# Query tiles 4 to 6 turned by DMA, and the last output tile stored in three pieces

## The chip, the cores and the metric

The program runs on one core of one Trainium2 chip. A core has a tensor engine (PE, with its weight loads shown apart as PEld), a vector engine (DVE), a scalar engine (ACT), a pool engine (POOL) and a sync engine (SP), which in this kernel only issues DMAs. Each engine works through its own list of instructions in order and waits on semaphores where it needs another engine's result. The metric is the device time of one execution in microseconds; lower is better.

## The reference

One transformer layer on 2048 tokens of width 576, in bfloat16. Cut to what matters:

```
x  = A_x                                   # 1 x 2048 x 576
q, k, v = layernorm(x) @ wq, wk, wv        # 32 heads of width 18
for s in range(4):                         # four segments of 512 tokens
    p     = softmax(q_s k_s^T / sqrt(18) + causal mask)
    a_dot = p v_s
    a_mem = phi(q_s) M / (phi(q_s) z + 1e-6)     # phi(t) = t + 1 if t > 0 else exp(t)
    o_s   = g a_mem + (1 - g) a_dot              # g = sigmoid(beta), one gate per head
    M, z += phi(k_s)^T v_s, sum(phi(k_s))
h   = x + o @ wo
out = h + gelu(layernorm(h) @ w1 + b1) @ w2 + b2  # 576 -> 4608 -> 576
```

## The kernel before

Tokens are cut into 16 tiles of 128 rows, and two tiles make a chunk (8 chunks of 256). Tile t of chunk c is t = 2c + tl. For each tile the kernel loads x, normalises it (statistics and scaling on DVE, the power of -1/2 on POOL), turns it so that the width lies on partitions, projects it to q, k and v (L984), copies the results out of PSUM with padding to 32 columns per head (L988 to L1008), and turns q and k again (the tiles QT and KT). Attention goes in "visits": scores for four units into one PSUM tile (L1109, 32-row tiling of the tensor engine), one long exponential on ACT (L1126), masks on POOL (L1130), and the product with v (L1149, column tiling). Then come the output projection, the second normalisation, the first feed-forward matmul (F1, L1388 with its last 64 rows apart in L1382), the gelu, and the second feed-forward matmul (F2, L1574), whose result is added to a row piece `hc` of h (L1578) and stored (L1581).

Two x tiles are loaded at the start into x_p (tiles 0 and 1) and two into x_b (tiles 2 and 3). Key tiles from 2 on are turned by a DMA transpose (L564); query tiles 0 to 6 are turned on the tensor engine by eight 128-column matmuls (L1026) and copied out by DVE (L1029), those from 7 on by a DMA transpose.

F1 has a contraction of 576 = 4 x 128 + 64. Two halves of a pair can do their 64-row remainders side by side in a 64-row tiling: an operation called "rest" (four matmuls of L1382), followed by the 128-row ones (L1388). A change between full, row, column and 64-row tiling is a change of mode.

All work is written as operations `op(engine, duration, function, reads, writes)` by generators that a small planner runs; the planner numbers the operations as it makes them. The engines do not follow the planner, though: the list `ORDER` names all operations by number, and they are issued in just that order, so `ORDER` sets the order of every engine's instructions. `PLACE` says which of three PSUM banks an operation's bank is, and `FLIP` names the copies that go to the other of DVE and ACT than planned. SP issues all DMAs in its order; a DMA also waits until the one eight places before it has landed.

Numbers in `ORDER` that the prediction speaks of: 0 and 1 load x_p, 8 and 9 load x_b, 2 loads the query weights, 4 the key weights, 5 and 3 the last 64 rows of the key and query weights, 6 the value weights; 33 and 38 scale tiles 0 and 1 (L881); 102 and 136 turn them on PE (L904), 103 and 137 copy them out (L962); 104 and 105 are the statistics of tile 2, the first of x_b (L868); 155 and 158 are the first projections of tiles 0 and 1, 160 and 162 the next of tile 0, 180 the turning of its q, 192 the first scores; 27 writes the column of ones of the first v tile (L735), 208 to 211 compute 1 - g (L845), 249 is the first product with v. 360, 458 and 604 turn query tiles 4, 5 and 6 on PE, and 361, 459 and 605 copy them out. 81 is a filler matmul (L1633), issued where PE would idle early on.

Of the kernel before, what the change touches and what calls it, by code (L numbers as in the profile page):

```python
# [16 lines left out]
def kernel(  # L17
# [15 lines left out]
    nc = tc.nc  # L33
# [102 lines left out]
    class Tok(tuple):  # L136
# [21 lines left out]
    }  # L158
    FLIP = {
# [357 lines left out]
    def op(eng, dur, issue, rd=(), wr=(), slack=0.0, table=None, port=None, mode="full", tag=None):  # L517
# [7 lines left out]
        o.needs = needs  # L525
# [419 lines left out]

    def stream_P(tl, chunks):
        for c in chunks:
# [65 lines left out]
            for dst, dk, g0, parts in ((QTs[t % NQ], ("QT", t % NQ), 0, (0, 2)), (KTs[t % NK], ("KT", t % NK), G, (1, 2))):  # L1013
# [14 lines left out]
                op("PE", 0.45, tr, pk + ["ident"], [b])  # L1028
                op("DVE", 0.69, lambda dst=dst, ptq=ptq: nc.vector.tensor_copy(out=dst[:], in_=ptq), [b], [dk])  # L1029
# [413 lines left out]
    def stream_F1():  # L1443
# [27 lines left out]
        for c in range(NCH):  # L1471
# [33 lines left out]
            while jp < NF // 2:  # L1505
# [18 lines left out]
                if pair:  # L1524
# [31 lines left out]
    def stream_F2():  # L1556
        for c in range(NCH):
            hT = hTs[c % 2]
            for tl in range(2):
                t = 2 * c + tl  # L1560
                for hf in range(2):
                    hs = slice(hf * HALF, (hf + 1) * HALF)
                    yield need(lambda: c in gelued, f_slots, [("hT", c % 2, 0)])
                    dma(144, 8, lambda t=t, hs=hs: nc.sync.dma_start(out=hc[:], in_=hd[t * P:(t + 1) * P, hs]), [("hd", t)], ["hc"], due("hc"))
                    b = f_slots.take()
                    for f in range(0, NF, 4):
                        hk = [("hT", c % 2, f // 2), ("hT", c % 2, f // 2 + 1)]
                        if f:
# [301 lines left out]
```

## Time and profile before

| what | value |
|---|---|
| median of 3 runs | 460.46 us (460.4 to 461.08) |
| the profiled execution's own time | 460.46 us |
| its span | 458.7 us |
| PE busy | 451.2 us (98%) |
| ACT busy | 332.2 us (72%) |
| DVE busy | 269.3 us (59%) |
| POOL busy | 223.2 us (49%) |
| mean DMA rate | 171 GB/s |

The span is what the profiler sees between the first and the last instruction; 1.8 us of the time lie around it. An engine's busy time is the union of its instructions. Matmuls are pipelined, so a matmul of 288 columns is listed with 286 ns from its start to its end, while the next one starts well before that end.

### The profile page before, as it was taken

The numbers are of one execution on the slowest core, as the hardware profiler recorded it, in microseconds if no ns is written. First come the engines' busy times: TensorE is split into PE (matmuls) and PEld (weight loads), VectorE is DVE, ScalarE is ACT, GpSimd is POOL, SyncE is SP. The second block draws the span as 40 slices with busy tenths as digits, with TensorE's granted clock in tenths as the row PEclk, the third lists the DMA queues.
The fourth block names the chain that finished last, engine by engine and source line by source line (L and its number), as shares of the span: only waits on it lengthen the run. The fifth ranks groups of instructions, "written<-read, shape, count | busy, mean of one in ns | idle before, by whom it ended". The sixth has DMA issues, their size and how long they took to land.

```text
span 458.7 us, 14406 instructions
## 1 busy us (share of the span) xinstructions
PE 451.2 (98%) x6066; PEld 333.2 (73%) x6066; DVE 269.3 (59%) x597; ACT 332.2 (72%) x331; POOL 223.2 (49%) x383
## 2 busy tenths in 40 slices
PE   8999999999999999999999999999999999999997
PEld 5656687576777766777677767777777878888875
DVE  5888798878576687877665587754643302231111
ACT  8788888996798977979679997697758533456400
POOL 5777775577767378875644578754312100000000
PEclk9999999999999999999999999999999999999999
DMA  8779997795595983948769857865657356782012
GB/s 227 145 180 278 253 262 165 214 216 123 154 217 149 226 155 95 203 146 194 166 122 178 211 160 183 205 182 167 174 171 184 103 167 196 206 251 77 27 40 64
DMA packets 112708, 78.40 MB, mean 171 GB/s; under 512 B 47187, under 2 KB 110595, under 8 KB 112643
## 3 DMA queue, kind: packets, MB, share of 16 engines
q1 hardware_dynamic: 112643, 77.48, 67.1%
q8 instruction: 47, 0.77, 0.7%
q14 instruction: 18, 0.15, 0.1%
HBM read 60.09 MB, written 7.08 MB: 146 GB/s over the span
## 4 chain that ended last, share of the span: by engine, by line
PE 90%; DMA 5%; DVE 2%; SPq 1%; issue 1%; ACT 1%; POOL 0%; DVEq 0%; ACTq 0%
PE bank L1574 23%; PE bank L1388 21%; PE bank L861 13%; PE last L1574 6%; PE st L1109 5%; PE ox L1149 4%; PE last L1388 4%; PE bank L1382 4%; PE bank L862 3%; PE ox L1574 2%; DMA x_b<-in_A_x_dram 1%; PE bank L1178 1%; DMA x_p<-in_A_x_dram 1%; DMA w1g<-in_B_w_dram 1%; PE ox L1388 1%; DMA xT<-xn 1%
## 5 line engine op out<-in xcount | busy, mean ns | idle before, releaser
L1126 ACT ACTIVATE pt<-st 128x2048 bf16<-128x2048 f32 x80 | 150.1, 1877 | 46.2 <-PE st L1109 39.9
L1574 PEld LDWEIGHTS <-hT 128*128 128x128 bf16 x1152 | 110.8, 98 | 28.4 <-issue 0.6
L1574 PE MATMUL bank<-w_sb,hT 128*128 128x288 bf16 x864 | 124.3, 286 | 0.0
L1464 DVE TENSOR_TENSOR hT<-bank,b1T 128x512 bf16<-128x512 f32 x96 | 64.8, 686 | 66.6 <-PE bank L1388 65.2
L1130 POOL TENSOR_SCALAR_AFFINE_SELECT pt<-pt 128x512 bf16<-128x512 bf16 x128 | 80.4, 640 | 40.2 <-ACT pt L1126 39.9
L1388 PE MATMUL bank<-xn2T,w1g 128*128 128x256 bf16 x768 | 96.4, 273 | 0.0
L1388 PEld LDWEIGHTS <-w1g 128*128 128x128 bf16 x864 | 80.3, 98 | 19.0 <-issue 9.1
L1480 ACT ACTIVATE hT<-hT 128x1536 bf16<-128x1536 bf16 (+4 forms) x25 | 66.0, 2666 | 2.0 <-DVE hT L1464 1.8
L861 PE MATMUL bank<-wqkv,xT 128*128 128x432 bf16 (+2 forms) x256 | 55.9, 341 | 0.9 <-DVE h_t L1315 0.3
L861 PEld LDWEIGHTS <-xT 128*128 128x128 bf16 x392 | 35.5, 98 | 22.0 <-issue 1.7
L1462 ACT ACTIVATE hT<-bank,b1T 128x256 bf16<-128x256 f32 x46 | 19.1, 472 | 22.6 <-PE bank L1388 17.6
L1168 POOL TENSOR_TENSOR pq<-ek,pq 128x512 bf16<-128x512 bf16 x24 | 27.7, 1154 | 11.6 <-DVE ek L1166 11.3
L1109 PE MATMUL st<-QT,KT 32*128 32x128 bf16 x1280 | 32.2, 217 | 0.2 <-ACT pt L1126 0.2
L1574 PE MATMUL last<-w_sb,hT 128*128 128x288 bf16 x216 | 31.0, 286 | 0.0
L1109 PEld LDWEIGHTS <-KT 32*128 32x128 bf16 x1280 | 18.6, 92 | 15.4 <-issue 11.4
L1193 DVE STREAM_TRANSPOSE ox<-ox 128x512 f32<-128x512 f32 x32 | 23.1, 723 | 9.2 <-PE ox L1149 9.2
L1149 PE MATMUL ox<-pt,v_aug 128*19 128x128 bf16 x1280 | 25.8, 220 | 0.8 <-DVE v_aug L735 0.8
L1149 PEld LDWEIGHTS <-v_aug 128*19 128x19 bf16 x1280 | 17.9, 91 | 9.6 <-issue 6.5
L1578 DVE TENSOR_TENSOR ot<-bank,hc 128x288 bf16<-128x288 f32 x24 | 10.9, 453 | 23.2 <-PE bank L1574 14.9
L1164 POOL TENSOR_SCALAR pq<-QT 128x512 bf16<-128x512 bf16 x24 | 14.7, 614 | 17.9 <-PE bank L1178 17.4
L1332 POOL TENSOR_TENSOR h_t<-h_t,b_bc 128x576 f32<-128x576 f32 x16 | 20.5, 1284 | 3.3 <-ACT xn L889 1.8
L862 PE MATMUL bank<-wqkv,xT 65*128 65x432 bf16 (+2 forms) x64 | 21.9, 343 | 0.0
(146 smaller groups left out, 629.2 us busy)
## 6 DMA issues: line engine op xcount, KB each, us to landing
w1g<-in_B_w_dram SPq DMA_DIRECT2D x57, 512.0 KB, 3.8
w_sb<-in_B_w_dram SPq DMA_DIRECT2D x6, 864.0 KB, 7.7
wqkv<-in_B_w_dram SPq DMA_DIRECT2D x10, 512.0 KB, 4.6
hd<-h_t SPq DMA_DIRECT2D x16, 288.0 KB, 3.3
hc<-hd SPq DMA_DIRECT2D x32, 144.0 KB, 2.8
w1g<-in_B_w_dram SPq DMA_DIRECT2D x114, 32.0 KB, 3.4
x_b<-in_A_x_dram SPq DMA_DIRECT2D x18, 144.0 KB, 3.5
hT<-in_B_w_dram SPq DMA_DIRECT2D x5, 512.0 KB, 4.0
```

Of the source, the lines that this page charges most:

```text
L861: nc.tensor.matmul(out=out_ap, lhsT=lhsT_of(slice(0, P), k), rhs=rhs_of(slice(0, P), k), start=(k == 0), stop=False)
L862: nc.tensor.matmul(out=out_ap, lhsT=lhsT_of(slice(0, rest), 4), rhs=rhs_of(slice(0, rest), 4), start=False, stop=True)
L1109: nc.tensor.matmul(out=st4[:, i, n * P:(n + 1) * P], lhsT=KTs[(2 * (c - c % 2) + kt) % NK][rows, g, :], rhs=QTs[(2 * c + qt) % NQ][rows, g ...
L1126: op("ACT", 1.88, lambda: nc.scalar.activation(out=pt[:], in_=st4[:], func=ACT.Exp, scale=scale), sk, [("pt", slot, n) for n in range(4)], ...
L1130: op("POOL", 0.65, lambda n=n: nc.gpsimd.affine_select(out=pt[:, :, n * P:(n + 1) * P], in_=pt[:, :, n * P:(n + 1) * P], pattern=[[0, 4], ...
L1149: nc.tensor.matmul(out=ox[32 * i:32 * i + E, (g % 4) * P:(g % 4) * P + P], lhsT=v_augs[(2 * s0 + kt) % NV][:, G * i + g, :], rhs=pts[slot] ...
L1168: op("POOL", 1.16, lambda: nc.gpsimd.tensor_tensor(out=pq[:], in0=e_g, in1=pq[:], op=ALU.add), ["ek"], ["pq"], slack=due("add"))
L1193: op("DVE", 0.73, lambda: nc.vector.transpose(out=ox[:], in_=ox[:]), [], ["ox"], slack=slack)
L1388: nc.tensor.matmul(out=self.acc[:, a, :], lhsT=self.wt[:, k, f:f + P], rhs=xn2T[self.c % 4][:, k, :], start=False, stop=(k == 3), skip_gro ...
L1464: either((0.684, lambda: nc.vector.tensor_tensor(out=dst, in0=acc(), in1=bias, op=ALU.add)), (nj * (0.22 + w * 0.00098), by_act), [b, "b1T ...
L1480: op("ACT", (f1e - f0) * Q * 0.00083 + 0.18, lambda: nc.scalar.activation(out=hT[:, f0:f1e, :], in_=hT[:, f0:f1e, :], func=ACT.Gelu_apprx_ ...
L1574: nc.tensor.matmul(out=bank_of(b)[:, 0:HALF], lhsT=hT[:, q, tl * P:(tl + 1) * P], rhs=w2_sb[:, q, hs], start=(q == 0), stop=(q == NF - 1))
```

## The change

Query tiles 4, 5 and 6 are turned by a DMA transpose that SP issues, in place of eight matmuls and a DVE copy each. The second half of the last token tile's output (288 columns) is computed as two pieces of 144 columns, each with its own 36 matmuls, its own addition and its own store; the first half is stored by itself as soon as it is added, so the tile leaves in pieces of 288, 144 and 144 columns. A new set `WHOLE` names 23 of the 47 "rest" operations that are left out: their halves do the 64-row remainder as a fifth full matmul. `PLACE`, `FLIP` and the whole of `ORDER` are new. The numbers in `ORDER` are the same as before up to 2509; behind that the last tile has twelve more operations (2510, 2522 and 2533 are the three stores, 2511 the load of hc, 2512 to 2520 and 2523 to 2531 the matmuls of the two small pieces, 2521 and 2532 their additions).

```diff
     PLACE = {
...
     FLIP = {
...
+    WHOLE = {
+        2534, 2535, 2537, 2538, 2539, 2540, 2541, 2542, 2544, 2548, 2550, 2551, 2552, 2557, 2560, 2561, 2565, 2567,
+        2568, 2569, 2570, 2571, 2575,
+    }
...
-                op("PE", 0.45, tr, pk + ["ident"], [b])
-                op("DVE", 0.69, lambda dst=dst, ptq=ptq: nc.vector.tensor_copy(out=dst[:], in_=ptq), [b], [dk])
+                o = op("PE", 0.45, tr, pk + ["ident"], [b])
+                turned_q[t, g0] = o, op("DVE", 0.69, lambda dst=dst, ptq=ptq: nc.vector.tensor_copy(out=dst[:], in_=ptq), [b], [dk]), lambda dst=dst, g0=g0, qk2d=qk2d: (
+                    nc.sync.dma_start_transpose(out=dst[:], in_=qk2d[:, g0 * P:(g0 + G) * P]))
...
-                            half.ops.append(op("PE", 4 * mm(Q), lambda half=half, a=a: half.main(a), pair.keys, [half.b]))
+                            half.ops.append(op("PE", 4 * mm(Q), lambda half=half, a=a: half.main(a) if half.rest or not half.pair.parted else half.whole(a), pair.keys, [half.b]))
...
+                ending = t == 2 * NCH - 1
...
+                    w = HALF // 2 if ending and hf else HALF
+                    for lo in range(hf * HALF, (hf + 1) * HALF, w):
...
+                        op("DVE", 0.45 if w == HALF else 0.27, lambda b=b, hs=hs, own=own, w=w: nc.vector.tensor_tensor(
+                            out=ot[:, hs], in0=bank_of(b)[:, 0:w], in1=hc[:, own], op=ALU.add), [b, "hc"], [key], slack=due("ot"))
+                        f_slots.give(b)
+                        if ending:
+                            dma(w // 4, 8, lambda t=t, hs=hs: nc.sync.dma_start(out=of[t * P:(t + 1) * P, hs], in_=ot[:, hs]), [key], (), due("out"))
+                if not ending:
+                    dma(144, 8, lambda t=t: nc.sync.dma_start(out=of[t * P:(t + 1) * P, :], in_=ot[:]), [("ot", 0), ("ot", 1)], (), due("out"))
...
         def go():
             for a in range(2):
                 for half in two:
-                    half.tail(a)
+                    if half.rest:
+                        half.tail(a)
...
-            h.rest = o
+            h.rest = o.made not in WHOLE and o
...
+    for (t, g0), (a, b, go) in turned_q.items():
+        if t >= 4:
+            a.eng, a.dur, a.issue, a.toks, a.gone_pe = "SP", 1.25, go, [], True
...
     ORDER = [
-        1, 11, 23, 19, 52, 0, 81, 73, 64, 81, 44, 81, 2, 81, 26, 81, 49, 8, 81, 81, 46, 5, 81, 81, 34, 81, 62, 3, 81,
-        22, 65, 29, 81, 66, 18, 4, 81, 47, 30, 81, 81, 9, 61, 21, 81, 67, 31, 68, 81, 35, 10, 32, 56, 81, 81, 36, 55,
-        6, 81, 81, 37, 63, 33, 81, 7, 81, 81, 15, 59, 81, 38, 54, 102, 109, 25, 136, 51, 230, 81, 20, 103, 81, 81,
-        81, 104, 155, 45, 137, 48, 105, 158, 58, 106, 156, 107, 138, 160, 159, 139, 205, 140, 162, 24, 141, 166, 161,
...
+        0, 26, 21, 25, 1, 19, 60, 81, 2, 81, 81, 53, 18, 5, 81, 81, 50, 81, 59, 3, 81, 29, 64, 81, 51, 8, 81, 44, 22,
+        81, 30, 11, 81, 4, 56, 81, 31, 65, 81, 34, 66, 9, 20, 81, 67, 68, 81, 32, 23, 35, 259, 81, 55, 81, 24, 81,
+        16, 49, 69, 81, 81, 33, 10, 36, 45, 102, 28, 37, 6, 104, 48, 81, 81, 78, 81, 81, 103, 70, 81, 38, 81, 7, 105,
+        136, 54, 155, 137, 62, 106, 158, 63, 107, 46, 79, 81, 81, 108, 159, 138, 162, 14, 139, 143, 205, 160, 140,
+        199, 156, 141, 166, 76, 161, 73, 163, 164, 167, 184, 185, 206, 27, 168, 142, 165, 182, 186, 144, 180, 169,
...
+        2525, 2507, 2508, 2513, 2514, 2509, 2515, 2516, 2511, 2517, 2526, 2510, 2518, 2527, 2528, 2519, 2520, 2529,
+        2530, 2521, 2531, 2522, 2532, 2533,
```

More of the change, by code (lines that the diff above doesn't have):

```diff
@@ L524, in op @@
         o.toks = [k for k in (*rd, *wr) if isinstance(k, Tok)]
-        o.needs = needs
+        o.needs, o.keys, o.gone = needs, (rd, wr), False
         o.port = eng == "POOL" if port is None else port
@@ L1560, in stream_F2 @@
                 t = 2 * c + tl
+                ending = t == 2 * NCH - 1
                 for hf in range(2):
-                    hs = slice(hf * HALF, (hf + 1) * HALF)
                     yield need(lambda: c in gelued, f_slots, [("hT", c % 2, 0)])
[L1564 to L1568, printed above, removed]
-                            yield need(None, None, hk)
-                        work["F2"] += 0.5
-                        def go(f=f, b=b, hT=hT, tl=tl, hs=hs):
-                            for q in range(f, f + 4):
-                                nc.tensor.matmul(out=bank_of(b)[:, 0:HALF], lhsT=hT[:, q, tl * P:(tl + 1) * P], rhs=w2_sb[:, q, hs],
-                                                 start=(q == 0), stop=(q == NF - 1))
-                        op("PE", 4 * mm(HALF), go, hk + [("w2", f // 6), ("w2", (f + 3) // 6)], [b])
@@ L1700 @@
             rest([halves[c, jp], halves[c, jp + 1]])
-    ORDER = [
[131 rows of a table removed]
+    for (t, g0), (a, b, go) in turned_q.items():
+        if t >= 4:
+            a.eng, a.dur, a.issue, a.toks, a.gone_pe = "SP", 1.25, go, [], True
+            a.needs = [d for d in a.needs if getattr(d, 'tag', ' ')[0] != "ident"] + [d for d in b.needs if d is not a]
+            a.start = a.end = b.start
+            d = Op("DMA", 256 / DMA_RATE + LAG[256], None, (), 0.0)
+            d.first, d.n, d.kb, d.toks, d.start, d.end = 1.3, 64, 256, (), a.start, a.start + 2
+            a.moves = d
+            for o in ops:
+                if b in o.needs:
+                    o.needs = [x for x in o.needs if x is not b] + [d]
+                elif a in o.needs and o is not b:
+                    o.needs = o.needs + [d]
+            b.gone, b.toks = True, []
+    ORDER = [
[132 rows of a table added]
     ]
```

24 lines of the change are left out of this document (20 added, 4 removed), and 284 rows, old and new, of tables (FLIP, ORDER, PLACE).

## The prediction

> **What bounds the kernel now.** First the page: its engine table, the granted clock and the chain that ended last.
>
> ```profile
> span 458.7 us, 14406 instructions
> PE 451.2 (98%) x6066; PEld 333.2 (73%) x6066; DVE 269.3 (59%) x597; ACT 332.2 (72%) x331; POOL 223.2 (49%) x383
> PEclk9999999999999999999999999999999999999999
> PE 90%; DMA 5%; DVE 2%; SPq 1%; issue 1%; ACT 1%; POOL 0%; DVEq 0%; ACTq 0%
> ```
>
> The tensor engine is the bound: 98% busy at full clock and 90% of the chain. So a change is worth what it does to the list of PE's instructions, to the moment at which PE can start on it, and to the few waits inside it. The view of PE's waits shows how few these are (in all: us, times, longest):
>
> ```profile
> PE ox L1149 <- DVE v_aug L735: 0.8, 1, 0.8
> PE bank L904 <- DVE xn L881: 0.4, 1, 0.4
> PE ox L1026 <- DVE qk_pad L992: 0.3, 1, 0.3
> PE bank L861 <- DVE h_t L1315: 0.3, 1, 0.3
> PE bank L861 <- DMA wqkv<-in_A_wk_dram: 0.2, 1, 0.2
> ```
>
> Of the five left, four are 0.2 us each and one is the wait of a filler. What the new order could win by waiting less is thus about 3 us, nearly all before 90 us; what it could lose is open. I therefore read three things: the start, PE's list, the end.
>
> **The start.** SP's timeline, start and duration, and below it the time from issue to landing of the small weight loads of L731:
>
> ```profile
> 0.79 0.88 SPq L727 DMA_DIRECT2D x_p<-in_A_x_dram  x2
> 1.71 0.43 SPq L730 DMA_DIRECT2D wqkv<-in_A_wq_dram  x1
> 2.19 0.51 SPq L727 DMA_DIRECT2D x_b<-in_A_x_dram  x1
> 2.73 0.56 SPq L731 DMA_DIRECT2D wqkv<-in_A_wk_dram  x1
> 3.34 0.58 SPq L731 DMA_DIRECT2D wqkv<-in_A_wq_dram  x1
> ...
> DMA to landing us min/median/max: 5.5/5.6/5.7
> ```
>
> The timelines of DVE and of PE over the same stretch:
>
> ```profile
> 5.79 0.43 DVE L881 TENSOR_SCALAR xn<-x_p,mv_p,rstd_p 128x576 bf16<-128x576 bf16 x1 [0.73 <-POOL rstd_p L873]
> 6.68 0.43 DVE L881 TENSOR_SCALAR xn<-x_p,mv_p,rstd_p 128x576 bf16<-128x576 bf16 x1 [0.47 <-POOL rstd_p L873]
> 8.12 0.46 DVE L868 BATCH_NORM_STATS2 stats_p<-x_b 128x6 f32<-128x288 bf16 x1 [0.19 <-DMA x_b<-in_A_x_dram]
> ```
>
> ```profile
> 7.17 0.45 PE L904 MATMUL bank<-ident,xn 128*128 128x128 bf16 x5 [0.38 <-DVE xn L881]
> 7.46 0.60 PE L1633 MATMUL st<-pq 128*128 128x256 bf16 x4
> 7.99 0.90 PE L861 MATMUL bank<-wqkv,xT 128*128 128x432 bf16 x4
> 9.04 0.89 PE L861 MATMUL ox<-wqkv,xT 128*128 128x432 bf16 x4
> 10.33 0.89 PE L861 MATMUL bank<-wqkv,xT 128*128 128x432 bf16 x4 [0.21 <-DMA wqkv<-in_A_wk_dram]
> 14.30 0.61 PE L1026 MATMUL ox<-ident,qk_pad 128*128 128x128 bf16 x8 [0.30 <-DVE qk_pad L992]
> 16.48 0.40 PE L1109 MATMUL st<-QT,KT 32*128 32x128 bf16 x16
> ```
>
> Before, DVE scales tile 1 (38) at 6.68, PE turns it (136) at 7.17 and projects tile 0 (155) from 7.99 on; the first x_b tile is looked at later, at 8.12, when it has just landed. The new `ORDER` changes two places. SP issues x_b (8) sixth instead of fourth, behind 5 and 3. And DVE gets 104, the statistics of that x_b tile, ahead of 38. DVE works in order, so tile 1 now waits behind a load. The first six transfers are the same six, so the sixth lands when the sixth landed before: 3.34 + 5.5 = 8.8 us. Then 104 runs 8.8 to 9.25, 38 to 9.7, 136 starts at 9.7 and takes 0.28 (five matmuls at 0.056, below), and 155, which stands behind 136 on PE, starts at 10.0: 2.0 us late. Not all is lost. The wait for the key weights (PE at rest until 10.33, some 0.4) is over by then, and so most likely is the one at 14.30 (0.3 to 0.45). Counting on from 10.0 with the durations of before (two fillers of 0.1 each stand between), the first scores (192) come at 17.7 instead of 16.48: **+1.2 us**. Bounds: 0, if x_b lands by 6.7 after all, and +2.0, if nothing is won back. I take 1.2, since the landing is bounded by the row of a transfer in the same place. The value weights (6) also go out later on SP, behind three small loads and a landing that SP must await; their first reader (190) stands right ahead of 192, at about 16.8 now, and I cost this at nothing with that cover, and at what the landing is late past 16.8 if the cover is gone.
>
> **The 24 us stretch.** DVE's timeline before:
>
> ```profile
> 22.91 1.69 DVE L845 TENSOR_SCALAR omg<-g_bc 32x8 f32<-32x8 f32 x3
> 24.76 0.09 DVE L735 MEMSET v_aug<- 128x32 bf16 x1 [0.16 <-issue]
> ```
>
> The column of ones (27) stood behind the slow L845 instructions, and PE waited 0.8 for it. The new list has 27 early, so this goes: -0.8. Late next are the copies out of PSUM on DVE (262, 236, 189), which now stand behind those same L845 instructions; PE needs their banks for 233 and 263 and their data for 279. By the durations above these come some 0.4 and 0.8 us late. I take 0 for the stretch, bounds -0.8 and +0.8.
>
> **PE's list.** Rows of the chain in order of time (start, duration, what):
>
> ```profile
> 18.82 0.45 PE bank L1026 x8
> 125.97 0.98 PE bank L1574 x8
> ...
> 127.28 1.09 PE bank L1574 x8
> 128.37 0.33 PE bank L1382 x4
> 128.69 0.98 PE bank L1388 x8
> 130.16 0.87 PE bank L1388 x8
> 448.15 7.36 PE bank L1574 x60
> ```
>
> Turning a query tile takes PE 0.45 us; three go: -1.35. Eight matmuls of L1574 take 0.98 us, and 1.09 behind a change of mode; eight of L1388 take 0.87 and 0.98. So a change of mode costs 0.11, and a "rest" 0.33 with the change into it, its four matmuls alone thus 0.22. A half pair without it does four full 256-column matmuls more, 4 x 0.87 / 8 = 0.44. Of the 23 left out, 10 stand between full-mode work in the old list: they save 0.22 and two changes and add 0.44, nothing. 13 have a neighbour in another mode: they save one change, 0.33, and add 0.44: 13 x 0.11 = +1.4. Counted in the two lists, mode changes fall from 284 to 254; the 23 account for 33, so the order itself adds 3: +0.3. The small pieces: 60 matmuls of 288 columns take 7.36 us, 0.123 each; eight of 128 columns take 0.45, 0.056 each; 144 columns are then 0.063 (an estimate between these rows), and 72 x 0.063 against 36 x 0.123 is +0.1. Sum of PE's list: -1.35 + 1.4 + 0.3 + 0.1 = **+0.5**. Bounds: the whole price of the 23 is between 0 and 23 x 0.11 = 2.5, so -0.9 to +1.6.
>
> One row speaks to a harsher price of the 144-column matmuls, the weight load:
>
> ```profile
> L1574 PEld LDWEIGHTS <-hT 128*128 128x128 bf16 x1152 | 110.8, 98 | 28.4 <-issue 0.6
> ```
>
> If a load of 98 ns had to end between two matmuls, 72 would take 7.1 us, +2.6. But the transposes above load weights for each matmul too and run at 56 ns, so the loads overlap; I stay with 0.063. The Trainium skill (TensorE: Matmul & The Clock Gate, section Back-to-back issue gap) says that in a stream of weight load and matmul pairs a 128-column matmul takes about 81 ns, not 56. By its figure 72 x 0.081 would make the pieces +1.4 instead of +0.1; this trace disagrees, with 0.45 us for eight.
>
> **Work moved to SP, DVE and the queues.** From the views of the lines:
>
> ```profile
> L564 SPq DMA_TRANSPOSE QT<-qk_pad x9: 1232/1694/2299, 95.8 to 290.9; - x9
> DMA to landing us min/median/max: 3.1/3.8/4.4
> ...
> L1029 DVE COPY QT<-bank x6: 625/680/691, 19.4 to 82.5; 128x1024 bf16<-128x1024 bf16 x6
> ```
>
> SP issues three more transposes of 1.2 to 2.3 us, each landing 3.8 later. Summing PE's list, the first scores that read tiles 4, 5 and 6 follow more than 20 us behind the old turning, so the latency is hidden. Behind each on SP stand a key transpose or weight loads; PE has no wait on those of more than 0.2. I take +0.1 for the crowding, bounds 0 and 3 x 0.3 = +0.9 (each costing the wait of the L861 rows above). DVE loses three copies of 0.68, PSUM a bank; neither is the bound: 0, at best a wait of 0.3.
>
> **The end.** DVE and SP timeline:
>
> ```profile
> 455.54 0.46 DVE L1578 TENSOR_TENSOR ot<-bank,hc 128x288 bf16<-128x288 f32 x1 [2.48 <-PE bank L1574]
> 456.03 0.34 SPq L1581 DMA_DIRECT2D out_dram<-ot  x1
> ```
>
> The last addition has half the columns: about 0.3 instead of 0.46. The store issue of 0.34 stays, with as many rows. The new list loads hc (2511) ahead of the first store (2510), and the first small piece is done three groups (0.75 us) ahead of the second, so its store is off SP by then. I take **-0.2**, bounds -0.5 and +0.4 (one store issue in front of the last). A quarter of the row is 288 bytes. The Trainium skill (DMA: Bandwidth & Descriptors, section Specifications) says that transfers under 512 bytes become a read-modify-write; a slower last store would eat that 0.2. No run here shows it yet.
>
> **Sum.** +1.2 + 0 + 0.5 + 0.1 - 0.2 = +1.6. The profiled execution took 460.46 us (1.8 around its span), which is also the median of the runs, so 460.46 + 1.6 = 462.1. The measured spread is 0.7 us; 0.2%, 0.9 us, is about what this kernel's times can tell from no change.
>
> **Rivals.** (a) Faster: x_b lands by 6.7, when DVE would have turned to 38. The start then costs 0, and the column of ones gives -0.8. With PE's list +0.5 and the end -0.2 that is -0.5; if most of the other listed waits behind the start (0.3 and four of 0.2, 1.1 in all) go too, -1.3: 459.2. It decides at a landing of x_b before 6.7; against it stands the row at 8.12, where even the fourth place was only just in. (b) Given back: PE is late, but so its later waits shrink: -1.1, the same five, against +1.6: 461.0. For it: these waits end on DMAs and DVE work that need not be late. Against it: most sit on engines that wait for PE in turn. (c) Worse: the crowded queue and the copies behind L845 both bite, +0.9 and +0.8 more: 463.8, and with the 98 ns loads beyond it.
>
> **How the numbers follow.** Forecast 0.53, (a) 0.20, (b) 0.15, (c) 0.12. The first and the last are slower by over 0.2%: 0.65; (b) is the same; (a) faster. The range runs from (a)'s 459.2 to 464.2, a little past (c), and leaves out about 2 in 10; the forecast's own range is 461.2 to 463.0.
>
> **What would show it.** Right: tile 1 scaled after 9 us, 155 at about 10.0, 192 at about 17.7, no wait on v_aug at 24 us, 23 groups of four L1382 fewer, the 144-column matmuls at 63 ns, the last addition at 0.3. Wrong: 155 before 8.5, or waits of PE behind 30 us that shrink by more than a microsecond.

## The result and the profile after

| | median | lowest to highest | runs |
|---|---|---|---|
| before, measured beside it | 460.92 us | 460.4 to 462.36 | 6 |
| after | 466.25 us | 465.61 to 467.73 | 6 |

The ratio is 1.0113, with a 95% interval of 1.0094 to 1.0133: the change makes the kernel slower by 5.3 us. The direction was forecast, the size was not: 462.1 was predicted, and 466.25 lies outside the range.

From the page of the kernel after (its engine table, the granted clock, the chain):

```profile
span 464.2 us, 14445 instructions
PE 451.0 (97%) x6077; PEld 339.7 (73%) x6077; DVE 267.1 (58%) x597; ACT 333.3 (72%) x335; POOL 223.8 (48%) x379
PEclk9999999999999999999999999999999999999999
PE 91%; DMA 6%; SPq 1%; issue 1%; DVE 1%; ACT 0%; DVEq 0%
```

PE is busy for as long as before (451.0 against 451.2) in a span that is 5.5 us longer. So most of the loss is waiting, not work of PE. The view of PE's waits of the kernel after (in all: us, times, longest; the row left out is the wait of a filler, 1.7 us against 1.3 before):

```profile
PE bank L908 <- DVE xn L885: 2.8, 2, 2.2
PE bank L865 <- DMA xT<-xn: 2.8, 2, 2.1
...
PE st L1116 <- issue: 1.6, 2, 1.2
PE bank L866 <- DMA w1g<-in_B_w_dram: 0.5, 1, 0.5
```

The first row is the start, which was forecast. The next two, on the transposed x and on "issue", were not there before, and are not in the forecast at all. The wait on v_aug (0.8 before) is gone.

**The start** came as predicted. DVE's and PE's timelines of the kernel after:

```profile
8.74 0.46 DVE L872 BATCH_NORM_STATS2 stats_p<-x_b 128x6 f32<-128x288 bf16 x1 [2.28 <-DMA x_b<-in_A_x_dram]
9.12 0.41 DVE L885 TENSOR_SCALAR xn<-x_p,mv_p,rstd_p 128x576 bf16<-128x576 bf16 x1
```

```profile
9.59 0.45 PE L908 MATMUL bank<-ident,xn 128*128 128x128 bf16 x5 [2.24 <-DVE xn L885]
9.88 0.89 PE L865 MATMUL bank<-wqkv,xT 128*128 128x432 bf16 x4
17.63 0.40 PE L1116 MATMUL st<-QT,KT 32*128 32x128 bf16 x16
```

DVE stands in front of the statistics of x_b until 8.74, tile 1 is scaled at 9.12 (before: 6.68), and the first scores come at 17.63 instead of 16.48. These are single executions. In the profiles of the five kernels below that keep this start, the statistics of x_b begin between 7.56 (late_no_q) and 8.91 us (after_loads_late), and the first scores come between 16.44 and 19.33; in those of the nine kernels with the old start, between 15.53 and 17.41.

**The wait for the transposed x.** SP's timeline of the kernel after, and below it two rows of its chain (start, duration):

```profile
22.23 0.98 SPq L1356 DMA_DIRECT2D hT<-in_B_w_dram  x2
23.26 0.59 SPq L753 DMA_DIRECT2D wo_t<-in_A_wo_dram  x1
23.89 1.08 SPq L1359 DMA_DIRECT2D w1g<-in_B_w_dram  x1
25.15 2.66 SPq L568 DMA_TRANSPOSE xT<-xn  x1
```

```profile
25.15 7.55 DMA xT<-xn
35.22 5.88 DMA xT<-xn
```

The transpose of tile 4's x (242) is issued at 25.15 and lands 7.55 us later. PE waits 2.3 us for it from 30.4 on, and 0.7 us for the next one at 40.3 (taken from the start of one matmul to the start of the next; the view counts from the end of the one, so it shows a little less). Before, this transpose was issued at 22.45, and the two transposes of x in this stretch landed 4.2 and 4.7 us after their issue:

```profile
21.32 0.50 SPq L727 DMA_DIRECT2D x_b<-in_A_x_dram  x1
21.87 0.47 SPq L1352 DMA_DIRECT2D hT<-in_B_w_dram  x1
22.45 1.24 SPq L564 DMA_TRANSPOSE xT<-xn  x1
...
DMA to landing us min/median/max: 4.2/4.4/4.7
```

Its source is late as well (DVE scales tile 4 at 24.17 now), and two weight loads of 512 KB (230 and 258, the row at 22.23) stand just ahead of it. Neither is one of the three transposes of the change; the first of those is issued at 48.84.

**The wait for nothing.** In the third row shown PE waits for "issue", that is, for nothing that the semaphores show. PE's timeline of the kernel after:

```profile
62.60 0.28 PE L1116 MATMUL st<-QT,KT 32*128 32x128 bf16 x5
63.25 0.35 PE L1116 MATMUL st<-QT,KT 32*128 32x128 bf16 x11 [0.37 <-issue]
...
68.14 0.40 PE L1116 MATMUL st<-QT,KT 32*128 32x128 bf16 x14
69.72 0.23 PE L1116 MATMUL st<-QT,KT 32*128 32x128 bf16 x2 [1.18 <-issue]
```

Both times PE stops in the middle of a group of 16 matmuls, and its two stopping places lie exactly 256 instructions apart. The trace has a DMA queue of its own for instructions, with 47 packets of 16 KB for PE's 12,165 recorded instructions: one packet for about 256 of them:

```profile
q8 instruction: 47, 0.77, 0.7%
```

The packets before the two stops ran from 60.5 to 62.0 and from 67.25 to 68.3 us, and PE went on 1.25 and 1.4 us behind their ends. Before, the first of these packets left at 57.1, and PE never stopped. In each of the nine kept traces that show such a wait, PE stops at one or both of these same two places of its list. So PE waited for its own instructions.

### The profile page after: what moved, and what is told of

The parts are those of the page before. It is cut to its first block, busy times and chain, and to the rows that moved or that the text cites. A ratio compares the mean times of both kernels' runs of the same rounds, so it can differ in the third digit from the quotient of the medians.

```text
span 464.2 us, 14445 instructions
## 1 busy us (share of the span) xinstructions
PE 451.0 (97%) x6077; PEld 339.7 (73%) x6077; DVE 267.1 (58%) x597; ACT 333.3 (72%) x335; POOL 223.8 (48%) x379
## 4 chain that ended last, share of the span: by engine, by line
PE 91%; DMA 6%; SPq 1%; issue 1%; DVE 1%; ACT 0%; DVEq 0%
PE bank L865 23%; PE bank L1587 21%; PE bank L1395 12%; PE last L1587 6%; PE bank L866 6%; PE st L1116 6%; PE ox L1156 4%; PE last L1395 4%; DMA xT<-xn 3%; PE bank L1389 2%; PE ox L1587 2%; PE bank L1185 1%; DMA x_b<-in_A_x_dram 1%; PE ox L1395 1%; DMA w1g<-in_B_w_dram 1%; DMA hc<-hd 1%
## 5 line engine op out<-in xcount | busy, mean ns | idle before, releaser
L1587 PE MATMUL bank<-w_sb,hT 128*128 128x288 bf16 (+1 forms) x864 | 124.2, 284 | 0.0
L1471 DVE TENSOR_TENSOR hT<-bank,b1T 128x512 bf16<-128x512 f32 x89 | 60.6, 687 | 56.8 <-PE bank L1395 39.4
L865 PE MATMUL bank<-xn2T,w1g 128*128 128x256 bf16 (+1 forms) x424 | 57.1, 265 | 0.5 <-DVE ot L1593 0.3
L1395 PEld LDWEIGHTS <-w1g 128*128 128x128 bf16 x512 | 47.8, 98 | 11.0 <-issue 4.6
L1395 PE MATMUL bank<-xn2T,w1g 128*128 128x256 bf16 x416 | 52.8, 273 | 0.0
L1469 ACT ACTIVATE hT<-bank,b1T 128x256 bf16<-128x256 f32 x60 | 25.1, 470 | 31.0 <-PE bank L1395 28.0
L865 PEld LDWEIGHTS <-w1g 128*128 128x128 bf16 x432 | 39.1, 98 | 7.3 <-issue 0.9
L1587 PE MATMUL last<-w_sb,hT 128*128 128x288 bf16 (+1 forms) x252 | 34.1, 277 | 0.0
L866 PE MATMUL bank<-xn2T,w1g 128*128 128x256 bf16 (+1 forms) x106 | 28.0, 265 | 0.5 <-DMA w1g<-in_B_w_dram 0.5
L1593 DVE TENSOR_TENSOR ot<-bank,hc 128x288 bf16<-128x288 f32 (+1 forms) x24 | 10.7, 447 | 23.7 <-PE bank L1587 17.5
L1210 POOL TENSOR_TENSOR o_nat<-t,t 128x288 bf16<-128x288 f32 x24 | 19.6, 818 | 8.8 <-DVE t L1209 8.8
```

The lines of the kernel that those rows point to most:

```text
L865: nc.tensor.matmul(out=out_ap, lhsT=lhsT_of(slice(0, P), k), rhs=rhs_of(slice(0, P), k), start=(k == 0), stop=False)
L866: nc.tensor.matmul(out=out_ap, lhsT=lhsT_of(slice(0, rest), 4), rhs=rhs_of(slice(0, rest), 4), start=False, stop=True)
L1395: nc.tensor.matmul(out=self.acc[:, a, :], lhsT=self.wt[:, k, f:f + P], rhs=xn2T[self.c % 4][:, k, :], start=False, stop=(k == 3), skip_gro ...
L1469: nc.scalar.activation(out=dst[:, j, :], in_=acc()[:, j, :], func=ACT.Identity, bias=b1T[:, j0 + j:j0 + j + 1], scale=1.0)
L1471: either((0.684, lambda: nc.vector.tensor_tensor(out=dst, in0=acc(), in1=bias, op=ALU.add)), (nj * (0.22 + w * 0.00098), by_act), [b, "b1T ...
L1587: nc.tensor.matmul(out=bank_of(b)[:, 0:w], lhsT=hT[:, q, tl * P:(tl + 1) * P], rhs=w2_sb[:, q, hs], start=(q == 0), stop=(q == NF - 1))
```

## The experiments

In the tables and texts a ratio is always to the kernel before on the same chip (median 460.9 to 461.7 us, 16 to 27 runs).

**1. Which part?** Each of the three visible parts alone in the kernel before, and the start undone in the kernel after.

qdma_only is the kernel before with the three DMA transposes of the change in the places of the three turnings; 361, 459 and 605 leave `ORDER`.

```diff
+    for (t, g0), (a, b, go) in turned_q.items():
+        if t >= 4:
+            a.eng, a.dur, a.issue, a.toks, a.gone_pe = "SP", 1.25, go, [], True
...
-        386, 363, 361, 301, 387,
+        386, 363, 301, 387,
...
-        497, 476, 459, 464, 477,
+        497, 476, 464, 477,
...
-        589, 677, 605, 649, 370,
+        589, 677, 649, 370,
```

> The kernel before, with query tiles 4 to 6 turned by DMA at the same places of the list and nothing else changed. Theory ORDER (the loss comes from the rewritten order, not from the three DMAs): PE's list shrinks by 3 x 0.45 = 1.35 us and the waits stay as before, so about 459.5, 1 us faster than before (0.998). Theory CROWDING (the three DMA transposes themselves make the other transfers and the instruction fetches of PE late between 30 and 75 us): the 4 us of waits seen there in the changed kernel come back, so 462 to 464 (1.003 to 1.007), with waits of PE on xT or on nothing (issue) in that stretch.

whole_only is the kernel before with the 23 wholes (in the numbers of the old list, 12 less than in the new one):

```diff
+    WHOLE = {
+        2522, 2523, 2525, 2526, 2527, 2528, 2529, 2530, 2532, 2536, 2538, 2539, 2540, 2545, 2548, 2549, 2553, 2555,
+        2556, 2557, 2558, 2559, 2563,
+    }
```

> The kernel before, with the same 23 pairs of halves doing their 64-row remainder as full matmuls, nothing else changed. The prediction's sum: 10 pairs cost nothing, 13 cost 0.11 us each, +1.4, so 461.9 (1.003); its bounds 0 to +2.5. Rival: the rests also hold PE up (they need both banks), so leaving them out wins back waits: 460.0 to 460.5 (no change).

tail_only is the kernel before with the last tile in three pieces, and the new order from 2506 on:

```diff
+                ending = t == 2 * NCH - 1
...
+                    w = HALF // 2 if ending and hf else HALF
```

> The kernel before, with the last tile stored in pieces of 288, 144 and 144 columns, in the order that the change gives them. The prediction's sum: +0.1 for 72 matmuls of 144 columns instead of 36 of 288, -0.2 at the end, so -0.1 (460.8 where before is 460.9). Rival (weight loads bind at 144 columns): the 72 matmuls take 5.8 to 7.1 us instead of 4.4, so +1.2 to +2.5.

head_undone is the kernel after with the statistics of tile 2 (104, 105) behind the scaling of tile 1 (38):

```diff
-        37, 6, 104, 48, 81,
+        37, 6, 48, 81,
...
-        70, 81, 38, 81, 7, 105, 136, 54,
+        70, 81, 38, 104, 105, 81, 7, 136, 54,
```

> The changed kernel, with the statistics of tile 2 (104 and 105) put behind the scaling of tile 1 (38) on DVE; the list is otherwise that of the change. The prediction's step: 136 starts at about 7.2 instead of 9.6, the first scores about 1.2 us earlier than 17.6. If that is passed on, 465.0 (1.2 below the changed kernel). If the later waits on transfers (xT at 30 us) take it back, the time stays at 466 while the first scores are early.

| run | median | ratio | 95% interval |
|---|---|---|---|
| qdma_only | 467.32 | 1.013 | 1.0088 to 1.0171 |
| whole_only | 462.66 | 1.0021 | 0.9999 to 1.0043 |
| tail_only | 460.31 | 0.9976 | 0.9949 to 1.0003 |
| head_undone | 465.77 | 1.0091 | 1.0058 to 1.0125 |

The wholes and the pieces are about where the working had them. The start alone gives back 1.0 us or so, which its interval does not tell from nothing; in its trace PE then waits longer at 29.9 (2.7 us) for the same transposed x. The surprise is qdma_only: three transposes that take 1.35 us off PE's list cost 5.6 us. Its waits, of PE and of ACT:

```profile
PE bank L864 <- ACT qk_pad L994: 2.5, 2, 2.2
PE bank L864 <- DMA xT<-xn: 1.0, 1, 1.0
PE ox L1155 <- issue: 0.9, 1, 0.9
```

```profile
ACT qk_pad L994 <- DMA QT<-qk_pad: 3.1, 1, 3.1
```

The costliest is not a reader of the turned tile but the next writer of its source: the transpose of tile 6 is issued at 85.21 and lands after 91; until then ACT may not overwrite the padded q and k, and PE stands behind ACT. Then something else comes on top. The busy times by stretch (PE, PEld, DVE, ACT, POOL, then the granted clock, DMA share and GB/s) of qdma_only:

```profile
86.00:89.00 3.00, 2.73 (x29) 1.33 (x28) 2.72 (x8) 2.42 (x3) 1.65 (x2) 1.00 1.04 331
89.00:92.00 3.00, 0.91 (x5) 0.39 (x4) 1.56 (x5) 0.47 (x2) 2.29 (x6) 0.97 1.23 217
92.00:95.50 3.50, 3.40 (x11) 1.43 (x11) 1.34 (x3) 2.83 (x5) 0.16 (x1) 0.54 0.35 98
```

After a rest of 2.35 us the granted clock is 0.54 for the next 3.5 us; nine 432-column matmuls start 0.36 apart instead of 0.18, which costs another 1.45.

**2. Is it the place of the transposes, and is it they at all in the new order?**

q6_early is qdma_only with the transpose of tile 6 right behind the last reader of the old tile (563):

```diff
-        531, 557, 563, 532, 541,
+        531, 557, 563, 604, 532, 541,
...
-        639, 705, 604, 640, 568,
+        639, 705, 640, 568,
```

> The kernel before with query tiles 4 to 6 turned by DMA, as in qdma_only, but the transpose of tile 6 (604) is given to SP right behind the last reader of the old query tile (563), some 7 us earlier. In qdma_only ACT waits 3.1 us at 91.5 for this transpose before it may overwrite the padded q and k, PE then rests 2.35 us, and the granted clock is 0.54 from 92 to 95.5. Theory 'a late transpose holds its source': both go, 2.35 + 1.45 us, and the time falls from 467.3 to 463.5 (1.004 to before). Rival 'volume' (three more transposes in a full queue cost what they cost, wherever they stand): 466.5 to 467.5, the rest only moves.

q456_retimed is q6_early with 360 behind 363, and 458 right behind 427:

```diff
-        346, 348, 360, 352, 376,
+        346, 348, 352, 376,
...
-        378, 386, 363, 301,
+        378, 386, 363, 360, 301,
...
-        394, 309, 427, 420, 436,
+        394, 309, 427, 458, 420, 436,
...
-        505, 451, 458, 367, 508,
+        505, 451, 367, 508,
```

> As q6_early, and besides the transpose of tile 4 (360) behind the transposed x of tile 6 (363) on SP instead of ahead of it, and that of tile 5 (458) ahead of two of the three loads of 864 KB instead of behind them. Theory 'place': with the three costs of qdma_only gone (0.85 at 47, 1.4 at 60, 3.8 at 90) only the shorter list of PE is left, 1.35 us less: 460.3 (0.997 to before). If the waits at 60 are for PE's own instructions, which come late whenever 2.6 MB of loads and a transpose stand in the queues together, these 1.4 stay: 461.7 (1.000). Rival 'volume': 466.5 to 467.5.

after_no_q is the kernel after with the turnings on TensorE; 361, 459 and 605 come back right behind 360, 458 and 604, of which the last two stand a few places earlier, where a PSUM bank is free (`PLACE` has their banks):

```diff
-        if t >= 4:
+        if t >= 99:
...
-        391, 371, 360, 215, 413,
+        391, 371, 360, 361, 215, 413,
```

> The changed kernel with query tiles 4 to 6 turned on TensorE again (three turnings and three copies by DVE, at about the places in the new order where the DMAs stood). Theory 'the new order, not the transposes' (for the changed kernel): the waits for the transposed x at 30.4 (2.3 us) and 40.3 (0.7 us) stay, since they lie ahead of the first of the three; PE's list is 1.35 longer; of the waits for PE's own instructions at 62.7 and 68.5 (0.47 and 1.28) half may go. 466.2 to 467.6 (1.010 to 1.013 to before). Rival 'the transposes': without them the new order is about as fast as the old one with the early loss of 1.2 us and the 1.4 us of the wholes: 462 to 463.5 (1.001 to 1.004).

after_xT_first is the kernel after with two loads of 512 KB behind the transposed x of tile 4 (242):

```diff
-        225, 196, 230, 146, 237, 258, 202, 194,
+        225, 196, 146, 237, 202, 194,
...
-        52, 39, 272, 227, 211,
+        52, 39, 272, 230, 258, 227, 211,
```

> The changed kernel with the two loads of 512 KB that SP issues at 22.23 (230 and 258) moved behind the transpose of tile 4's x (242) and the load behind it. In the changed kernel this transpose is issued at 25.15, lands 7.55 us later, and PE waits 2.3 us for it; before it was issued at 22.45 and landed some 4 us later. Theory 'big loads just ahead in the queue': it lands within 4.5 us, the wait is at most 0.3 and the time falls from 466.25 to 464.2 (1.007 to before). Rival 'it is late anyway' (VectorE's scaling of tile 4 ends at 24.9 instead of 22.4, and the lost time is taken back by later waits): 465.5 or more.

| run | median | ratio | 95% interval |
|---|---|---|---|
| q6_early | 463.09 | 1.0047 | 1.0022 to 1.0072 |
| q456_retimed | 466.79 | 1.0121 | 1.0103 to 1.0138 |
| after_no_q | 467.49 | 1.0126 | 1.0098 to 1.0155 |
| after_xT_first | 467.77 | 1.0138 | 1.0112 to 1.0164 |

q6_early confirms the first reading: issued some 7 us earlier, the transpose of tile 6 holds nobody, and 3.8 us come back (by the ratios). (Its profiled run, at 466.25, is one of its slowest: it shows no ACT wait any more, but 2.3 us for a transposed x at 47.3 and half clock behind that. The fast runs of this kernel lie between 461.5 and 466.3, so the medians decide.) q456_retimed was meant to mend the other two and made things worse:

```profile
PE st L1115 <- issue: 2.0, 1, 2.0
PE bank L864 <- DVE h_t L1321: 1.7, 1, 1.7
PE ox L1155 <- issue: 1.5, 1, 1.5
```

With the transpose of tile 5 ahead of two loads of 864 KB instead of behind them, those loads come later, and now PE waits 3.5 us for its instructions. after_no_q says that in the new order the loss does not hang on the three transposes: without them it is as slow. In its trace no wait for instructions is left, but the early wait for x is 3.7 us, and PE pays for it twice (stretches of after_no_q, columns as above):

```profile
29.00:33.00 4.00, 0.48 (x9) 0.33 (x7) 2.77 (x7) 1.85 (x2) 2.73 (x6) 0.92 0.96 83
33.00:36.00 3.00, 2.86 (x41) 1.35 (x44) 0.00 (x0) 0.52 (x1) 0.58 (x1) 0.50 1.39 187
36.00:39.50 3.50, 3.50 (x40) 2.19 (x33) 1.86 (x4) 1.98 (x2) 1.22 (x2) 0.55 0.97 248
```

after_xT_first put the two loads behind the transpose, and the wait for x was gone: PE was 2.5 us ahead at 30. But the loads now stood ahead of others, and PE waited for those:

```profile
PE bank L865 <- DMA wo_t<-in_A_wo_dram: 2.1, 1, 2.1
PE st L1116 <- DMA KT<-hT: 1.6, 1, 1.6
```

**3. Loads that nobody needs yet.** In q6_early two loads of 864 KB put back, in the kernel after the two of 512 KB put back further, and a try at something faster than both kernels.

q6_w2late, against q6_early:

```diff
-        364, 432, 389, 424, 428,
+        364, 432, 424, 428,
...
-        428, 416, 431, 42, 425,
+        428, 416, 42, 425,
...
-        559, 530, 531, 557, 563,
+        559, 530, 531, 389, 431, 557, 563,
```

> q6_early with two of the three loads of 864 KB that stand ahead of the transpose of query tile 5 on SP (389 and 431, first read after 94 us) moved some 15 us later, behind the last load before SP's idle time. In q6_early the packet that brings PE's next instructions leaves at 63.1 and PE waits 1.1 us for it at 64.4; before it left at 57.1 and nothing waited. Theory 'PE's instructions wait behind the data that is in the queues': the packet leaves by 59 and this wait is under 0.2; the time falls by some 1.1 us, from 463.1 to 462.0 (1.0015 to before). Rival 'the third long transpose itself holds the packet up, whatever loads stand by it': the wait stays over 0.8 and the time at 463.1 (1.0047).

after_loads_late, against the kernel after:

```diff
-        225, 196, 230, 146, 237, 258, 202, 194,
+        225, 196, 146, 237, 202, 194,
...
-        303, 295, 283, 240, 296,
+        303, 295, 283, 230, 240, 296,
...
-        247, 355, 363, 379, 400,
+        247, 355, 363, 258, 379, 400,
```

> The changed kernel with the two loads of 512 KB (230 and 258, first read after 54 us) moved further back than in after_xT_first: 230 behind the turning of key tile 3 (283), 258 behind the transposed x of tile 6 (363), so that neither the transposes of tiles 4 and 5 nor the rows of wo and the key tile that PE waited for in after_xT_first stand behind them. Theory 'each transfer late is one that stands behind loads that nobody needs yet': the waits at 30.4 (2.3 us) and 40.3 (0.7 us) fall under 0.5 together, nothing takes their place before 45, and the time falls from 466.3 to 463.8 (1.006 to before). Rival 'the queues are full up to 70 us and a load put off only comes in the way of the next': the waits go, but those for PE's own instructions at 62 to 70 grow from 1.7 to over 3 us, and the time stays over 465.5 (1.009).

best_no_q, against tail_only:

```diff
-        227, 254, 208, 238, 40,
+        227, 254, 27, 208, 238, 40,
...
-        210, 211, 27, 213, 232,
+        210, 211, 213, 232,
```

> A try at a version ahead of both: the kernel before, with the last tile in pieces of 288, 144 and 144 columns as in tail_only, and the column of ones of the first v tile (27) written ahead of the four additions of 1 - g (208 to 211) on DVE instead of behind them. The wait of PE for v_aug (0.84 us at 23.8) goes, and the end gives 0.1 to 1.1 us, as in tail_only. If nothing takes it back: 459.7 to 460.5 (0.996 to 0.998 to before). If what is won at 24 is waited for again at the transposed x of 31 us (0.34 us before, then 1.0): 461 (0.999).

best_q6, against best_no_q; 605 leaves `ORDER` and 604 stands as in q6_early:

```diff
+        if t == 6:
+            a.eng, a.dur, a.issue, a.toks, a.gone_pe = "SP", 1.25, go, [], True
...
-        531, 557, 563, 532, 541,
+        531, 557, 563, 604, 532, 541,
```

> best_no_q with query tile 6 alone turned by DMA, issued early as in q6_early; tiles 4 and 5 stay on TensorE. PE's list is 0.45 us shorter. Theory 'a transpose is free where its source is written early and nothing urgent stands behind it': 0.45 us below best_no_q, 459.2 to 460 (0.995 to 0.997). Rival 'every further transpose between 40 and 95 us costs about 1.8 us' (a third of the 5.5 of qdma_only): 461 to 462.5 (1.000 to 1.003).

| run | median | ratio | 95% interval |
|---|---|---|---|
| q6_w2late | 467.75 | 1.0157 | 1.0124 to 1.0191 |
| after_loads_late | 464.43 | 1.0085 | 1.006 to 1.0109 |
| best_no_q | 461.06 | 1.0003 | 0.9979 to 1.0028 |
| best_q6 | 462.96 | 1.0047 | 1.0026 to 1.0068 |

In q6_w2late the two loads are out of the way, and no wait for "issue" is left, though the same three transposes are there. So the loads have a part in making the instructions late. It is nevertheless the slowest of all by the ratio, because a weight load that PE needs at 80 us now stands behind them:

```profile
PE bank L1388 <- DMA hT<-in_B_w_dram: 4.8, 1, 4.8
```

The transposes alone do not make the wait for "issue", then. The loads alone made none in the kernel before, but a short one in whole_only, which has the old loads and none of the three transposes:

```profile
PE ox L1155 <- issue: 0.5, 1, 0.5
```

In the old order it is 0.9 to 1.0 us in the traces of qdma_only and q6_early, with both. So the transposes add to it, and are not needed for it.

In after_loads_late the wait at 30.4 is gone and half a microsecond is left at 39, now on a result of DVE; its three longest waits are others:

```profile
PE bank L908 <- DVE xn L885: 2.4, 1, 2.4
PE st L1651 <- DVE pq L799: 1.7, 1, 1.7
PE st L1116 <- issue: 1.6, 2, 1.2
```

Of the 2.3 and 0.7 expected, 1.3 arrives in the time (by the ratios, with intervals that overlap). Part of the rest can be seen in this trace. PE rests 2.4 us at the late start, and the granted clock is then 0.50 for 3.4 us (columns as above):

```profile
9.50:12.90 3.40, 3.13 (x13) 1.68 (x14) 1.89 (x6) 0.00 (x0) 0.79 (x2) 0.50 0.85 238
```

That is some 1.7 us lost, and the first scores come at 19.33. The profiled run took 465.57 us at a mean clock of 0.996, as one other of the six did; the four with 0.999 or more took 463.9 to 464.9.

best_no_q does not beat the kernel before. The wait on v_aug goes, but PE then waits at 32.22 for a DVE result that cost 0.17 before:

```profile
32.22 0.89 PE L864 MATMUL bank<-wqkv,xT 128*128 128x432 bf16 x4 [1.30 <-DVE MZacc L1087]
```

best_q6, one transpose more, comes out 1.9 us above that, as the rival had it. Its profile shows 1.8 us for a transposed x at 48, which lies ahead of the only transpose that was added; so where these 1.9 us come from stays open.

**4. Do the parts add up?** Starting from after_loads_late: the three transposes undone, the start undone, and both.

late_no_q, with the turnings in `ORDER` as in after_no_q:

```diff
-        if t >= 4:
+        if t >= 99:
```

> after_loads_late with query tiles 4 to 6 turned on TensorE again, as in after_no_q. It asks what the three transposes are worth in the new order once the early wait for x is gone. Theory 'the transpose of tile 5 beside the loads of 864 KB makes PE's instructions late': the waits for them at 62 and 68 (0.5 and 1.3 us) go, as they did in after_no_q, PE's list is 1.35 longer, and the time is that of after_loads_late within 0.6: 463.9 to 464.6 (1.006 to 1.008 to before). Rival 'the transposes cost as in qdma_only': 460.5 to 462 (0.999 to 1.002). Rival 'they gain what they take off PE's list': 465.8 (1.010).

late_head, the edit of head_undone:

```diff
-        37, 6, 104, 48, 81,
+        37, 6, 48, 81,
...
-        70, 81, 38, 81, 7, 105, 136, 54,
+        70, 81, 38, 104, 105, 81, 7, 136, 54,
```

> after_loads_late with the statistics of tile 2 (104, 105) behind the scaling of tile 1 (38) again, as in head_undone. Theory 'the start's loss counts once nothing behind it waits': 137 still stands behind 104 and 105, so of the 1.2 us some 0.5 are won, as in head_undone: 463.9 (1.006). Rival 'taken back whole': 464.4 (1.0075 to 1.0085).

late_head_no_q has the edits of both:

```diff
-        if t >= 4:
+        if t >= 99:
...
-        70, 81, 38, 81, 7, 105, 136, 54,
+        70, 81, 38, 104, 105, 81, 7, 136, 54,
```

> Both of these together: the changed kernel with its early loads put off, the start mended and no query tile turned by DMA. What is left of the change is the 23 wholes (+1.0 as measured), the pieces at the end (0 to -1), the column of ones (-0.8) and the rest of the order. If the steps add up: 462 to 463.5 (1.002 to 1.005); above 464.5 something in the new order that I haven't named costs more than 1 us.

| run | median | ratio | 95% interval |
|---|---|---|---|
| late_no_q | 462.82 | 1.0051 | 1.0027 to 1.0075 |
| late_head | 462.35 | 1.0036 | 1.0015 to 1.0057 |
| late_head_no_q | 462.75 | 1.0034 | 1.0019 to 1.005 |

late_head is the key: with the start and the loads mended together 3.5 us come back, from 1.0113 down to 1.0036, more than either theory on record had (463.9 or 464.4 us). Mended one at a time, the start gives 1.0 us (head_undone) and the loads 1.3. But each edit was made in three surroundings, and all have to be read together (us by the ratios, each uncertain by some 1.5 us by the intervals):

| edit | in the kernel after | with the other mended | with the turnings on TensorE |
|---|---|---|---|
| the two loads put off | 1.3 | 2.5 (late_head against head_undone) | 3.5 (late_no_q against after_no_q) |
| the start undone | 1.0 | 2.3 (late_head against after_loads_late) | 0.8 (late_head_no_q against late_no_q) |

So the loads are worth some 2.4 us and the start some 1.4. That the two cover for each other is not shown: the 1.2 us by which 3.5 exceeds 1.0 and 1.3 lies within the noise of the four ratios. The loads alone are shown most clearly by late_no_q against after_no_q, which differ in nothing else and whose intervals lie apart. The waits of late_head and its start:

```profile
PE bank L908 <- DVE xn L885: 1.2, 2, 0.7
PE st L1116 <- issue: 1.2, 1, 1.2
PE bank L865 <- DMA xT<-xn: 0.6, 1, 0.6
```

```profile
7.87 0.45 PE L908 MATMUL bank<-ident,xn 128*128 128x128 bf16 x5 [0.52 <-DVE xn L885]
8.16 0.89 PE L865 MATMUL bank<-wqkv,xT 128*128 128x432 bf16 x4
```

The mean clock tells the same: 1.0 in every run of late_head; 0.996 in all six of head_undone; in the six of the kernel after, 0.996 in three, 0.993 in one and 1.0 in two. A mean of 0.996 over 464 us is 3.7 us at half clock, some 1.9 us lost.

The transposes themselves are then worth nothing either way: late_head and late_head_no_q are 0.4 us apart by the medians, 0.1 by the ratios. They take 1.35 us off PE's list, and a wait of 1.2 us for instructions comes with them. With the start late they cost 1.6 (late_no_q against after_loads_late, intervals that overlap), which lies between the two theories that had them cost much or nothing. What is left in late_head_no_q, 1.6 us, is the 23 wholes (1.0) and, net of what the end and the column of ones give, 0.6 without a name; since the wholes' own interval is 0 to 2 us, that may be nothing.

## Why the prediction was right and wrong, step by step

| step | predicted | in the trace after |
|---|---|---|
| start | +1.2 | +1.15 (17.63 against 16.48) |
| 24 us stretch | 0 | -0.8 |
| PE's list | +0.5 | +0.65 to +0.8 |
| work moved to SP, DVE and the queues | +0.1 (0 to 0.9) | +3.0 for x, +1.7 for instructions, +1.4 behind 90 us, half of it on DVE |
| other waits that shrink (rival b) | 0 in the forecast | -1.5 to -1.9 |
| end | -0.2 | -0.2 |

PE's list is the sum of what the parts alone did to it (qdma_only -1.1, whole_only +1.75, tail_only +0.2), or, a little less, what the trace of the kernel after holds when all longer waits are taken out. The waits in the last column are the start-to-start distances of consecutive matmuls, less what they are where nothing is waited for, summed over the stretch; the small ones depend on where a wait is told from a slow matmul, hence the two values.

**What bounds the kernel** was right: PE, and most of the loss is in what PE waits for.

**The start** was right in mechanism and size: x_b was looked at at 8.74 (8.8 predicted), 136 began at 9.59 (9.7), 155 at 9.88 (10.0), the first scores at 17.63 (17.7). That one execution meets the forecast within 0.1 us is luck, since in the other traces with this start the statistics begin up to 1.2 us earlier or 0.2 later. By the middle values, 17.45 against 16.14, the loss is 1.3. The bounds had no term for the clock: in after_loads_late the same start cost 2.9 us against the trace before, beyond the bound of 2.0.

**The 24 us stretch**: the wait on v_aug went and the copies behind the slow DVE instructions cost PE nothing; the true -0.8 is one end of the bounds. best_no_q shows that this gain is not robust: in the old order it was given back at 32 us.

**PE's list**: the counts were right (92 half-height matmuls fewer, 24 matmuls for turning fewer), and so was the 144-column matmul: the distances between them in the last tile have a mean of 62.5 ns, against 63. The weight load of 98 ns does not bind. So the figure of the Trainium skill (TensorE: Matmul & The Clock Gate, section Back-to-back issue gap), 81 ns for 128 columns with a weight load each, does not hold here. The wholes were sized about right: 1.75 us by the distances in the trace of whole_only and 1.0 by the ratio, whose interval is 0 to 2, against 1.4.

**The end** came as predicted: from the end of the last matmul to the end of the span it is 3.0 us, before 3.2. The Trainium skill's remark on transfers under 512 bytes (DMA: Bandwidth & Descriptors, section Specifications) shows no cost here: in the view of the DMA issues (count, KB each, median us to landing) the pieces with 288 bytes to a row land sooner than the whole tiles. They carry a quarter of the bytes, though, so a small cost isn't ruled out.

```profile
out_dram<-ot SPq DMA_DIRECT2D x15, 144.0 KB, 3.4
...
out_dram<-ot SPq DMA_DIRECT2D x2, 36.0 KB, 1.5
```

**The step that failed is the one on the queues.** "I take +0.1 for the crowding, bounds 0 and 3 x 0.3" rested on two sentences. "The latency is hidden" asked only who reads the turned tile. It did not ask who waits to overwrite its source, nor what else uses the queues: PE's own instructions do. And "PE has no wait on those of more than 0.2" took the waits of the old order as a bound for the new one. The working looked at the three transposes that were moved, and for the start at the first six transfers; it never laid the old and the new order of SP's loads side by side between 15 and 60 us. There two 512 KB loads, first read after 54 us, had gone ahead of a transpose that PE needed at 30. That, together with the late start, is 3.5 of the 5.3 us (late_head), and none of it is in the few words that name the change. So the term of +0.1, bounded by 0.9, stands against some 6 us of waits, of which the waits that shrank took back 1.5 to 1.9. Rival (c) had the direction, a crowded queue, but the same bound of 0.9.

**Rival (b)** came true in part. Seven waits of PE between 31 and 244 us, of 0.25 to 0.45 us each, are gone in the trace after. That is more than the microsecond that the prediction named as a sign of being wrong. It hid that much of what the queues cost. That PE's lateness is what made them shrink isn't shown: in late_head_no_q, where the start is mended, PE's waits are few as well.

## What to carry to other kernels

When the order of the DMAs changes, list for each stretch what stands ahead of every transfer that the bounding engine needs next, in the old and in the new order, with sizes; a load that nobody reads for 30 us is harmless only if nothing urgent stands behind it. For an operation that becomes a DMA, ask also who waits to overwrite its source. And make the same edit in more than one surrounding: putting off the two loads gave 1.3, 2.5 and 3.5 us in three of them, and the first alone, with intervals that overlap, would have said little.

## What the runs showed of the hardware

- **PE's instructions come by DMA and can be late.** One packet of 16 KB brings about 256 of PE's instructions; in the kernel after PE waited 0.5 and 1.3 us for two of them, in q456_retimed 1.5 and 2.0, in whole_only, without the three transposes, 0.5. The Trainium skill (DMA: Bandwidth & Descriptors, section Queues, rings and completion order) has each DMA engine go round its queues packet by packet, so that an instruction packet would wait for little more than one packet of data. By the runs it depends on the loads in the queues: without two of them the wait was gone (q6_w2late). No row shows when the packet was asked for, so where it is held up stays open.
- **A rest of some 2 us can halve PE's clock behind it.** After 2.35 us of rest the granted clock was 0.54 for 3.5 us (qdma_only), after 2.4 us it was 0.50 for 3.4 us (after_loads_late), after 3.7 us it was 0.50 to 0.55 for 6.5 us (after_no_q). After 2.0 us it was 0.50 from 70.1 to 73.5 (q456_retimed). After 2.3 us in the profiled run of the kernel after it stayed at 1.00, and the mean clock of four other runs of that kernel is below 1. The Trainium skill (TensorE: Matmul & The Clock Gate, section What's actually happening) names a window of about 3.4 us that runs freely and does not begin anew with a kernel. The length of the half-clock stretches in qdma_only and after_loads_late and the change from run to run agree with that; a drop after a rest shorter than the window goes beyond what it says.
- **A DMA transpose has no fixed price.** Transposes of padded q, all of the same shape, took SP 1.2 to 6.1 us to issue (q6_early, 56.04) and 3.1 (before) to 10.5 us (qdma_only, q6_early) from the start of the issue to the landing. The two longest stood behind three loads of 864 KB.
